# Routing product, row buffers, logits and FFN steps moved in a fused attention, FFN and expert kernel

## The chip, the cores and the metric

One core of a Trainium2 chip runs the kernel. The metric is the device time of one execution in microseconds (us), the median of several runs; a profiled execution of the same program gives the trace. Engines: PE (TensorE, matrix products), DVE (VectorE), ACT (ScalarE), POOL (GpSimd) and SP (SyncE, which only issues transfers).

## The reference

Three layers in a row, all in float32:

- Attention over `q`, `k`, `v` of shape 4 x 8 x 576 x 64: scores `q k^T / 8`; those under the row's maximum less `tau` are masked; softmax; times `v`. The result is laid out as 2304 tokens of 512 values.
- A dense FFN: `h = x @ w_in` (512 to 2048), `g = max(0.01 h, h)`, `x = g @ w_out`.
- A routed FFN: `logits = x @ w_gate + modality_bias[modality_id]` over 8 experts; each token goes to the expert with the largest logit, with that expert's softmax value as its gate: `out = gate * (relu(x @ w1[e]) @ w2[e])`, with 1024 hidden values.

## The kernel before, in words

The order of the instructions on each engine is written out by hand: every engine runs its own in program order and waits on semaphores where data comes from another engine. Products are made of a high and a low half of each float32 operand, so an operand is first copied (the high half, on ACT) and subtracted (the low half, on DVE or POOL).

**Attention** (`Attention`) goes over 16 pairs of heads in 9 steps each; a loop in `body` drives it. Products of probabilities and values (`pv`) come five steps late (`PVL`), and their evictions later still (`pv_out`: ACT in the following step, DVE in the one after), so there are some steps after the last score. Beside it `Units` runs the first part of the dense FFN for six blocks of 256 tokens, a few products per step (`start`, `mid`, `late`, `tail`), and `Moe1.convs` turns the dense weights into halves in small steps. What is left of the units at the end is run by `un.finish`, with one step of the weight conversion per round.

**The rest of the dense FFN** (`Tail`) is a list of items. An item is one slice of 128 hidden values: the first product `mm1` into `h`, the activation (`leaky`: ACT, DVE, ACT, DVE), and two items later (`LAG`) the second product `mm2` into `y`. First come blocks 6 to 8 with slices 0 to 5 (18 items), then all blocks with slices 6 to 15: blocks 0 to 7 in pairs, 512 columns wide (40 items), then block 8 alone (10 items). Then come two groups of 256 tokens of the most loaded experts (`turn` for tag `g`, 16 items), and after them the table-driven groups (`Groups`).

`pre` holds the steps to be done ahead of an item, by its place in the list: `fetch` asks SP for a block's rows of the attention result `xd` into the one buffer `un.xr`; `turn` transposes them on PE (`turned`, into PSUM tile `tp`) and makes the halves (`split_x`). `fetch_part` brings back the partial result of slices 0 to 5; for the last block that is done in `done1` itself, on SP, with the addition on DVE right behind.

**Routing** runs in the gaps. `extra` is a queue of generators; at each *place* (`advance`: between parts of `mm1`, after it, between parts of `mm2`, at the item's end; eight in a wide item, four in a narrow one) the first of them makes one step. `slowly(gen, k)` puts k places between two steps. When a block of `y` is done (`done1`), its logits and its routing are queued:

- blocks counted 1 to 6: `Route.logits`, 16 long vector operations with a running sum on DVE, one per place (`LD`);
- blocks 7 to 9: `Route.logits_mm`, eight transposes of `y` on PE into `ytp`, copies to `yT` (one on ACT, one on DVE; the tiles are `ct[2]` and `ct[0]`, of which `ct[0]` also serves the wide `leaky`), and 16 small product instructions into `lp`, with two places per step (`LG`);
- all: `Route.block`: the expert's one-hot row `hot` on DVE, then at the next place the product `rp` of `hot` with a triangle and with ones on PE (ranks and counts), then rank, gate and position `pi` on DVE, a store of `y` to `yd` on SP, and two scatters of token ids into `idt` from POOL, where the second waits for the first.

After block 9 `Route.table` makes the table of groups from the counts; its first group reads `idt` (`load_ids`), gathers rows of `yd` (`exg`) and is transposed on PE (`tp<-ident,exg`).

PSUM tag `u` has two buffers, which `tp`, `ytp`, `lp` and `rp` share in turn.

Of the kernel before, what the change touches and what calls it, by code (L numbers as in the profile page):

```python
# [31 lines left out]
GT = 256  # L32
# [423 lines left out]
class Route:  # L456
# [104 lines left out]
    def block(self, b, y, sb, ps, ps_tag):  # L561
# [23 lines left out]
        v.tensor_tensor(hot, per_e(self.w8), per_tile(fe), op=ALU.is_equal)  # L585
        yield
        rp = ps.tile([P, 512], F32, tag=ps_tag, name="rp")
# [14 lines left out]
        v.tensor_copy(pi, pf)  # L602
        nc.sync.dma_start(self.yd[b * GT:(b + 1) * GT, :].rearrange("(t p) c -> p t c", t=2), y)
        for t in range(2):
# [138 lines left out]
class Tail:  # L743
# [8 lines left out]
    def __init__(self, tc, ctx, mo, rt, un, w1, w2, out, wts):  # L752
# [8 lines left out]
        self.raw = itertools.cycle(self.raws).__next__  # L761
        self.xr1 = un.xr
        self.xh = itertools.cycle([un.xh, bp.tile([P, 4, GT], F32R, name="xh")]).__next__
# [31 lines left out]
    def fetch(self, b):  # L795
        self.mo.xload(b, self.xr1)

    def turn(self, key, rows, t, wide=False):
        if t == 0:
            self.xs = self.x5() if wide else (self.xh(), self.xl())  # L800
        elif t == (3 if wide else 1):
            self.x[key] = self.xs
        tp = self.pr.tile([P, 4, P], F32, tag="u", name="tp")
        turned(self.tc.nc, rows[:, t % 2], tp, self.rt.ident)
        for _ in split_x(self.tc.nc, tp, *self.xs, t):
            pass
# [12 lines left out]
    def done1(self, b, ys, part):  # L819
        nc = self.tc.nc  # L820
        yt = self.yt()
        for t in range(2):
            if part == 2:
                nc.vector.tensor_tensor(yt[:, t, 0:DM], ys[t], self.xgs[b % 2][:, t, 0:DM], op=ALU.add)
            elif part:
                nc.sync.dma_start(yt[:, t, 0:DM], self.mo.yp[2 * b + t])
                nc.vector.tensor_tensor(yt[:, t, 0:DM], ys[t], yt[:, t, 0:DM], op=ALU.add)
            elif t == 0:
                nc.vector.tensor_copy(yt[:, t, 0:DM], ys[t])
            else:  # L830
                nc.scalar.activation(yt[:, t, 0:DM], ys[t], AF.Copy)
        if self.blocks == 0:
            self.rt.load_wide(self.raws[2:])
        self.blocks += 1
        if self.blocks == 1:
            self.extra.append(iter([None] * 12))
        if self.blocks <= NB - 3:
            self.extra.append(slowly(self.rt.logits(yt, self.sb, f(self.cts[2])), LD[self.blocks - 1]))
        else:
            self.extra.append(slowly(self.rt.logits_mm(yt, self.yT, self.pr, "u"), LG))  # L840
        self.extra.append(slowly(self.rt.block(b, yt, self.sb, self.pr, "u"), RB[self.blocks - 1]))
        if self.blocks == NB - 3:
            self.extra.append(self.rt.early(self.sb1))
            self.extra.append(self.routed())
        elif self.blocks == NB:
            self.extra.append(self.rt.table(self.sb2()))
# [62 lines left out]
    def ahead(self, g, p):  # L909

        a = [(0, 0, lambda: self.load_ids(g)), (p - 7, 1, lambda: self.gather(g)),
             (p - 2, 3, lambda: self.turn(("g", g), self.xg[g], 0)), (p - 1, 3, lambda: self.turn(("g", g), self.xg[g], 1))]
        def load(q):
# [291 lines left out]

LG = 2

# [5 lines left out]
LAT = ["678", "457"]  # L1213
RB = [1] * 9
LD = [1]*8
FL = [0, 2, 3, 4]
# [146 lines left out]
def body(tc, qkt, vt, tau, win, wout, mid, wg, wgt, mb, w1, w2, out):  # L1363
    nc = tc.nc
    with ExitStack() as top, tc.manual_schedule():
# [12 lines left out]
        with ExitStack() as c1:  # L1378
# [12 lines left out]
            for w in steps:  # L1391
                if w == "conv":
                    pace += CV[n // 36]
                    while pace >= 1.0 and cv.n < 8 * NA:
                        next(cv)
                        pace -= 1.0
                elif n >= 36:
                    if w == "start" and n % 36 == LATE:
# [25 lines left out]
        ta.sb2 = lambda: groups().sb  # L1424
        bank[0] = itertools.cycle(ta.pys[2:4]).__next__
        un.finish(cv)
        items, pre = [], []
# [3 lines left out]
        for b in range(len(FB), NB):  # L1431
            p = len(items)
            pre += [(p - 5, 0, 0, lambda b=b: ta.fetch(b))] + [(p - 2 + t, 0, 0, lambda b=b, t=t: ta.turn(b, un.xr, t)) for t in range(2)]
            items += [item(b, fi, start=fi == 0, stop=fi == NA - 1, ys=ta.pys[0:2], done=(lambda ys, b=b: ta.done0(b, ys)))
                      for fi in range(NA)]
# [4 lines left out]
        for b in range(0, NB - 1, 2):  # L1440
            p = len(items)
            for k in range(2):
                pre += [(p - 4 + 2 * k, 0, 0, lambda b=b, k=k: ta.fetch(b + k)), (p + 5, 0, 0, lambda b=b, k=k: ta.fetch_part(b + k))]
                pre += [(p - 2 + k, 0, 0, lambda b=b, t=2 * k + t: ta.turn((b,), un.xr, t, True)) for t in range(2)]
            items += [dict(item(b, fi, start=fi == NA, stop=fi == NF - 1, nt=4, done=(lambda ys, b=b: both(b, ys))), x=(b,))
                      for fi in range(NA, NF)]
        items[(NB - len(FB)) * NA]["hook"] = lambda: bank.__setitem__(0, lambda: None)
        b, p = NB - 1, len(items)
        pre += [(p - 4, 0, 0, lambda: ta.fetch(b))] + [(p - 2 + t, 0, 0, lambda t=t: ta.turn((b,), un.xr, t)) for t in range(2)]
        items += [dict(item(b, fi, start=fi == NA, stop=fi == NF - 1, done=(lambda ys: ta.done1(b, ys, 1))), x=(b,)) for fi in range(NA, NF)]  # L1450
        p = len(items)
# [90 lines left out]
```

## Time and profile before

| | |
|---|---|
| median of 3 runs | 1055.83 us (1049.67 to 1056.2) |
| profiled execution | 1056.48 us, span of its instructions 1054.8 us |
| PE busy | 935.5 us, 89% of the span |
| DVE, ACT, POOL busy | 744.8, 587.7, 428.6 us |
| instructions | 20411 |
| HBM read, written | 118.88 MB, 19.79 MB |

A busy share is a mean over stages with different limits: attention ends near 400 us, the dense FFN near 765 us, and the groups fill the rest. The times in the rows below are from the span's start.

### The profile page before, as it was taken

What the parts mean: (1) busy time and instruction counts of PE and PEld (TensorE: products, weight loads), DVE (VectorE), ACT (ScalarE), POOL (GpSimd) and SP (SyncE); (2) the same over time, 40 slices, a digit from 0 to 9 for tenths busy, and PEclk for the clock granted to TensorE, in tenths of its full rate; (3) what the DMA queues carried; (4) which work ended last, traced back from release to release, by engine and by line L of the source; (5) the groups of instructions that cost most, each with busy time, mean ns of one, the idle gap of its engine ahead of it and who ended that gap; (6) DMA issues with size and microseconds to landing.
All of it is one profiled execution on the core that took longest, in us unless ns stands there. A gap on an engine that the chain in (4) does not pass through costs nothing. (4 is left out here: it accounts for less than half of the span.)

```text
span 1054.8 us, 20411 instructions
## 1 busy us (share of the span) xinstructions
PE 935.5 (89%) x7001; PEld 816.3 (77%) x7001; DVE 744.8 (71%) x1842; ACT 587.7 (56%) x1165; POOL 428.6 (41%) x514
## 2 busy tenths in 40 slices
PE   4666789999998997999998987989979999999984
PEld 3565678989897896888886875868868999998963
DVE  7898988989898873776368483684547666565574
ACT  6687888988887873654222212122335556564473
POOL 3899988898888861322000000010112211221121
PEclk9788899999999998999999998999989999999998
DMA  8999999999999884553032133042585988665572
GB/s 217 204 227 240 227 250 213 212 226 220 201 209 242 176 155 142 172 180 120 21 120 43 38 80 41 1 100 81 104 189 157 336 305 280 231 241 169 159 267 107
DMA packets 262874, 181.96 MB, mean 173 GB/s; under 512 B 186258, under 2 KB 223254, under 8 KB 262744
## 3 DMA queue, kind: packets, MB, share of 16 engines
q1 hardware_dynamic: 251696, 160.53, 62.8%
q0 software_dynamic: 4736, 12.92, 3.7%
q10 hardware_dynamic: 6312, 6.94, 2.1%
q8 instruction: 61, 1.00, 0.4%
q14 instruction: 69, 0.57, 0.2%
HBM read 118.88 MB, written 19.79 MB: 131 GB/s over the span
## 5 line engine op out<-in xcount | busy, mean ns | idle before, releaser
L196 POOL TENSOR_TENSOR p<-p,p 128x512 f16<-128x512 f32 x144 | 170.0, 1180 | 0.0
L150 PE MATMUL s<-khh,qs 128*128 128x288 f32 x320 | 105.6, 344 | 51.7 <-DVE p L175 28.5
L429 ACT ACTIVATE ct<-h 128x256 f32<-128x256 f32 (+1 forms) x104 | 48.3, 465 | 150.1 <-PE h L421 146.6
L453 PE MATMUL y<-w,g 128*128 128x512 f32 x480 | 130.3, 407 | 0.0
L158 DVE TENSOR_REDUCE s<-s 128x1 f32<-128x576 f32 x144 | 109.4, 759 | 26.2 <-PE s L223 23.3
L431 DVE SCALAR_TENSOR_TENSOR h<-h,ct 128x256 f32<-128x256 f32 (+1 forms) x104 | 55.3, 532 | 97.8 <-ACT ct L429 97.5
L453 PE MATMUL y<-w,w 128*128 128x512 f32 x480 | 124.3, 410 | 0.0
L175 DVE SCALAR_TENSOR_TENSOR p<-s,tb,e 128x576 f32<-128x576 f32 x144 | 117.3, 815 | 8.9 <-ACT e L167 4.4
L605 POOL DMA_INDIRECT idt<-ids,pi x18 | 17.8, 990 | 259.6 <-DVE pi L602 161.9
L421 PE MATMUL h<-w,w 128*128 128x512 f32 x480 | 120.4, 399 | 0.0
L150 PEld LDWEIGHTS s<-khh,qs 128*128 128x128 f32 x320 | 66.4, 208 | 61.2 <-DVE p L175 18.8
L222 PE MATMUL s<-vs,pt 128*128 128x128 bf16 (+1 forms) x680 | 109.2, 229 | 3.6 <-DMA pt<-p 3.5
L453 PEld LDWEIGHTS y<-w,w 128*128 128x128 f32 x480 | 93.6, 197 | 20.9
L167 ACT ACTIVATE e<-s,tb 128x576 f32<-128x576 f32 x144 | 107.1, 744 | 4.6 <-DVE tb L162 4.5
L421 PEld LDWEIGHTS h<-w,w 128*128 128x128 f32 x480 | 91.3, 191 | 21.6 <-DVE w L412 0.2
L223 PE MATMUL s<-vs,pt 128*128 128x64 bf16 (+1 forms) x680 | 104.1, 198 | 0.0
L194 ACT ACTIVATE p<-p 128x576 f16<-128x576 f32 x144 | 99.4, 690 | 4.9 <-DVE tb L162 4.1
L150 PE MATMUL s<-kll,qs 128*128 128x288 f32 x320 | 96.7, 316 | 0.0
L453 PEld LDWEIGHTS y<-w,g 128*128 128x128 f32 x480 | 85.6, 191 | 14.2
L225 PE MATMUL s<-vs,pt 128*128 128x128 bf16 (+1 forms) x544 | 90.1, 226 | 0.0
L421 PE MATMUL h<-uxh,w 128*128 128x256 f32 x448 | 88.6, 296 | 0.7 <-ACT uxh L410 0.7
L421 PE MATMUL h<-exh,w 128*128 128x256 f32 (+1 forms) x448 | 87.0, 290 | 0.7 <-ACT exh L410 0.7
(247 smaller groups left out, 2348.3 us busy)
## 6 DMA issues: line engine op xcount, KB each, us to landing
cr<-w SPq DMA_DIRECT2D x36, 512.0 KB
raw_qk<-qkt SPq DMA_DIRECT2D x30, 576.0 KB
raw<-w SPq DMA_DIRECT2D x24, 512.0 KB
ur<-xd SPq DMA_DIRECT2D x18, 512.0 KB
eraw<-w SPq DMA_DIRECT2D x18, 512.0 KB
cr<-w_in SPq DMA_DIRECT2D x16, 512.0 KB
cr<-w_out SPq DMA_DIRECT2D x16, 512.0 KB
ur<-w SPq DMA_DIRECT2D x12, 512.0 KB
```

Of the source, the lines that this page charges most:

```text
L150: nc.tensor.matmul(s[:, j, 0:288], qf[:, c0:c0 + P], x[:, j * 288:(j + 1) * 288], start=(k == 0), stop=(k == len(ops) - 1))
L158: v.tensor_reduce(self.mq[n], self.sq[n], axis=AX.XY, op=ALU.min)
L167: self.tc.nc.scalar.activation(e, self.sq[n], AF.Exp, bias=self.mq[n][:, 1:2], scale=-1.0)
L175: self.tc.nc.vector.scalar_tensor_tensor(p, self.sq.pop(n), self.mq.pop(n)[:, 0:1], self.eq.pop(n), op0=ALU.is_le, op1=ALU.mult, accum_out ...
L194: nc.scalar.activation(pp[:, 0:S], p, AF.Copy)
L196: nc.gpsimd.tensor_tensor(pp[:, S + D:], p[:, 0:4 * P], pp[:, 0:4 * P], op=ALU.subtract)
L222: nc.tensor.matmul(o[r0:r1, 0:2 * D], hi, v12, start=(c == 0), stop=False)
L223: nc.tensor.matmul(o[r0:r1, D:2 * D], hi, vs[:, h, c, 2], start=False, stop=(c == 4))
L225: nc.tensor.matmul(o[r0:r1, 0:2 * D], pt[:, 5 + c, r0:r1], v12, start=False, stop=False)
L421: nc.tensor.matmul(h, w[:, 0, a, s], b[:, c], start=(n == 0), stop=(n == 11))
L431: nc.vector.scalar_tensor_tensor(h, h, 0.01, a, op0=ALU.mult, op1=ALU.max)
L453: nc.tensor.matmul(y, a[:, s], w[:, 1, b], start=start and k == 0, stop=stop and k == 2)
```

## The change

- `Route.block`: three places instead of one between `hot` and the product `rp`; the store of `y` is issued by POOL instead of SP.
- Two buffers for the FFN's rows: `un.xr` and a weight tile, by the block's parity. Both fetches of a pair stand five items ahead (before: four and two). The fetch of block 6 is issued before `un.finish`.
- Blocks counted 2, 4 and 6 take their logits by `logits_mm` on PE, one place per step (`LG = 1`); blocks 7 to 9 do too, behind eight empty places each.
- No unit work in attention's last two steps (149 and 150); `un.finish` does it afterwards.
- `turn` is split into `turn`, `turn_g` and `turn_in`, and `RB` and `LD` become plain numbers of the same value.

```diff
@@ Route.block
         v.tensor_tensor(hot, per_e(self.w8), per_tile(fe), op=ALU.is_equal)
-        yield
+        for _ in range(3):
+            yield
         rp = ps.tile([P, 512], F32, tag=ps_tag, name="rp")
...
-        nc.sync.dma_start(self.yd[b * GT:(b + 1) * GT, :].rearrange("(t p) c -> p t c", t=2), y)
+        nc.gpsimd.dma_start(self.yd[b * GT:(b + 1) * GT, :].rearrange("(t p) c -> p t c", t=2), y)
@@ Tail.__init__
-        self.xr1 = un.xr
+        self.xrs = [un.xr, f(self.raws[1]).rearrange("p (t c) -> p t c", t=2)]
@@ Tail
     def fetch(self, b):
-        self.mo.xload(b, self.xr1)
-
-    def turn(self, key, rows, t, wide=False):
+        self.mo.xload(b, self.xrs[b % 2])
+
+    def turn(self, b, t, wide=False):
+        key, rows = ("x", b // 2) if wide else b, self.xrs[b % 2]
+        t += 2 * (b % 2) if wide else 0
         if t == 0:
             self.xs = self.x5() if wide else (self.xh(), self.xl())
         elif t == (3 if wide else 1):
             self.x[key] = self.xs
+        self.turn_in(rows[:, t % 2], t)
+
+    def turn_g(self, g, t):
+        if t == 0:
+            self.xs = self.xh(), self.xl()
+        else:
+            self.x["g", g] = self.xs
+        self.turn_in(self.xg[g][:, t], t)
+
+    def turn_in(self, row, t):
         tp = self.pr.tile([P, 4, P], F32, tag="u", name="tp")
-        turned(self.tc.nc, rows[:, t % 2], tp, self.rt.ident)
+        turned(self.tc.nc, row, tp, self.rt.ident)
         for _ in split_x(self.tc.nc, tp, *self.xs, t):
             pass
@@ Tail.done1
-        if self.blocks <= NB - 3:
-            self.extra.append(slowly(self.rt.logits(yt, self.sb, f(self.cts[2])), LD[self.blocks - 1]))
+        if self.blocks <= NB - 3 and self.blocks % 2:
+            self.extra.append(slowly(self.rt.logits(yt, self.sb, f(self.cts[2])), LD))
         else:
+            if self.blocks > NB - 3:
+                self.extra.append(iter([None] * 8))
             self.extra.append(slowly(self.rt.logits_mm(yt, self.yT, self.pr, "u"), LG))
-        self.extra.append(slowly(self.rt.block(b, yt, self.sb, self.pr, "u"), RB[self.blocks - 1]))
+        self.extra.append(slowly(self.rt.block(b, yt, self.sb, self.pr, "u"), RB))
@@ module
-LG = 2
+LG = 1
-RB = [1] * 9
-LD = [1]*8
+RB = 1
+LD = 1
@@ body
-                elif n >= 36:
+                elif 36 <= n < 9 * B * HP + PVL:
                     if w == "start" and n % 36 == LATE:
                         un.add(2 * (n // 36 - 1))
                     getattr(un, w)(n % 9)
...
         bank[0] = itertools.cycle(ta.pys[2:4]).__next__
+        ta.fetch(len(FB))
         un.finish(cv)
...
-            pre += [(p - 5, 0, 0, lambda b=b: ta.fetch(b))] + [(p - 2 + t, 0, 0, lambda b=b, t=t: ta.turn(b, un.xr, t)) for t in range(2)]
+            pre += [(p - 5, 0, 0, lambda b=b: ta.fetch(b))] if p else []
+            pre += [(p - 2 + t, 0, 0, lambda b=b, t=t: ta.turn(b, t)) for t in range(2)]
...
-                pre += [(p - 4 + 2 * k, 0, 0, lambda b=b, k=k: ta.fetch(b + k)), (p + 5, 0, 0, lambda b=b, k=k: ta.fetch_part(b + k))]
-                pre += [(p - 2 + k, 0, 0, lambda b=b, t=2 * k + t: ta.turn((b,), un.xr, t, True)) for t in range(2)]
+                pre += [(p - 5, 0, 0, lambda b=b, k=k: ta.fetch(b + k)), (p + 5, 0, 0, lambda b=b, k=k: ta.fetch_part(b + k))]
+                pre += [(p - 2 + k, 0, 0, lambda b=b, k=k, t=t: ta.turn(b + k, t, True)) for t in range(2)]
```

## Rows read from the trace of the kernel before

**Rows 1.** The page, part 1: busy us (share of the span) xinstructions.

```profile
PE 935.5 (89%) x7001; PEld 816.3 (77%) x7001; DVE 744.8 (71%) x1842; ACT 587.7 (56%) x1165; POOL 428.6 (41%) x514
```

**Rows 2.** Waits of PE from 390 us on: us in total, times, longest.

```profile
PE rp L590 <- DVE hot L585: 15.6, 7, 2.7
PE tp L405 <- DMA ur<-xd: 11.0, 3, 5.0
PE ytp L548 <- DVE yt L827: 6.8, 1, 6.8
```

**Rows 3.** Timeline of PE, 550 to 566 us: start, us, what, [idle before <-releaser].

```profile
551.18 2.96 PE L421 MATMUL h<-w,w 128*128 128x512 f32 x12
...
559.37 0.21 PE L590 MATMUL rp<-hot,tri 128*128 128x8 bf16 x2 [2.43 <-DVE hot L585]
...
559.51 4.59 PE L421 MATMUL h<-w,w 128*128 128x512 f32 x12
```

**Rows 4.** Windows: stretch, us, busy PE, PEld, DVE, ACT, POOL, clock, DMA share, GB/s.

```profile
555.00:645.00 90.00, 80.53 (x345) 64.08 (x344) 63.61 (x198) 17.33 (x33) 7.69 (x8) 0.92 0.24 53
685.00:765.00 80.00, 73.85 (x420) 62.99 (x419) 51.43 (x175) 21.99 (x49) 8.69 (x9) 0.98 0.42 95
466.60:473.80 7.20, 7.14 (x36) 5.96 (x37) 4.74 (x9) 4.31 (x9) 2.59 (x2) 1.00 0.43 146
409.00:416.20 7.20, 6.46 (x29) 5.87 (x30) 3.10 (x6) 3.05 (x6) 1.28 (x1) 0.53 0.42 151
656.80:664.00 7.20, 7.20 (x25) 6.07 (x26) 1.98 (x3) 1.68 (x3) 0.00 (x0) 0.64 0.00 0
779.50:786.70 7.20, 7.20 (x31) 6.34 (x32) 3.46 (x7) 2.71 (x7) 0.00 (x0) 0.63 0.62 156
```

**Rows 5.** Timeline of SP and PE around two fetches of rows.

```profile
462.50 0.37 SPq L399 DMA_DIRECT2D ur<-xd  x1
...
466.66 1.07 PE L405 MATMUL tp<-ident,ur 128*128 128x128 f32 x8 [1.34 <-DMA ur<-xd]
...
646.23 0.36 SPq L399 DMA_DIRECT2D ur<-xd  x1
...
656.80 1.94 PE L405 MATMUL tp<-ident,ur 128*128 128x128 f32 x8 [5.04 <-DMA ur<-xd]
```

**Rows 6.** Timeline of PE, block 7's logits product.

```profile
739.31 1.85 PE L558 MATMUL lp<-wg,ct 128*128 128x8 f32 x16
```

**Rows 7.** Timeline of SP, DVE and PE, the last block, 762 to 830 us.

```profile
767.20 0.89 SPq L826 DMA_DIRECT2D yt<-yp  x2
...
778.74 1.41 DVE L827 TENSOR_TENSOR yt<-y,yt 128x512 f32<-128x512 f32 x2 [6.49 <-DMA yt<-yp]
...
779.48 1.11 PE L548 MATMUL ytp<-ident,yt 128*128 128x128 f32 x4 [6.82 <-DVE yt L827]
...
784.05 0.69 DVE L552 COPY ct<-ytp 128x512 f32<-128x512 f32 x1 [0.70 <-PE ytp L548]
```

**Rows 8.** Timeline of PE, ACT and SP, end of attention, 390 to 412 us.

```profile
399.28 5.12 PE L453 MATMUL y<-w,g 128*128 128x512 f32 x21
...
401.25 0.31 ACT L251 ACTIVATE xs<-s,rs 128x64 f32<-128x64 f32 x1 [0.40 <-ACT ct L1288]
...
404.40 0.36 SPq L399 DMA_DIRECT2D ur<-xd  x1
...
409.05 1.67 PE L405 MATMUL tp<-ident,ur 128*128 128x128 f32 x8 [4.65 <-DMA ur<-xd]
```

**Rows 9.** Tile `idt`: duration ns min/median/max, first and last start.

```profile
L605 POOL DMA_INDIRECT idt<-ids,pi x18: 954/958/1202, 560.9 to 800.9; - x18
```

**Rows 10.** Timeline of POOL and PE, from the last scatter to the first table group.

```profile
800.87 0.98 POOL L605 DMA_INDIRECT idt<-ids,pi  x1 [5.92 <-DMA idt<-ids,pi]
...
811.55 1.03 POOL L1050 DMA_INDIRECT exg<-yd,eid  x1 [0.30 <-issue]
...
820.57 0.60 PE L405 MATMUL tp<-ident,exg 128*128 128x128 f32 x4
```

More of the change, by code (lines that the diff above doesn't have):

```diff
@@ L911, in ahead @@
         a = [(0, 0, lambda: self.load_ids(g)), (p - 7, 1, lambda: self.gather(g)),
-             (p - 2, 3, lambda: self.turn(("g", g), self.xg[g], 0)), (p - 1, 3, lambda: self.turn(("g", g), self.xg[g], 1))]
+             (p - 2, 3, lambda: self.turn_g(g, 0)), (p - 1, 3, lambda: self.turn_g(g, 1))]
         def load(q):
@@ L1442, in body @@
             for k in range(2):
-                pre += [(p - 4 + 2 * k, 0, 0, lambda b=b, k=k: ta.fetch(b + k)), (p + 5, 0, 0, lambda b=b, k=k: ta.fetch_part(b + k))]
-                pre += [(p - 2 + k, 0, 0, lambda b=b, t=2 * k + t: ta.turn((b,), un.xr, t, True)) for t in range(2)]
-            items += [dict(item(b, fi, start=fi == NA, stop=fi == NF - 1, nt=4, done=(lambda ys, b=b: both(b, ys))), x=(b,))
+                pre += [(p - 5, 0, 0, lambda b=b, k=k: ta.fetch(b + k)), (p + 5, 0, 0, lambda b=b, k=k: ta.fetch_part(b + k))]
+                pre += [(p - 2 + k, 0, 0, lambda b=b, k=k, t=t: ta.turn(b + k, t, True)) for t in range(2)]
+            items += [dict(item(b, fi, start=fi == NA, stop=fi == NF - 1, nt=4, done=(lambda ys, b=b: both(b, ys))), x=("x", b // 2))
                       for fi in range(NA, NF)]
@@ L1448, in body @@
         b, p = NB - 1, len(items)
-        pre += [(p - 4, 0, 0, lambda: ta.fetch(b))] + [(p - 2 + t, 0, 0, lambda t=t: ta.turn((b,), un.xr, t)) for t in range(2)]
-        items += [dict(item(b, fi, start=fi == NA, stop=fi == NF - 1, done=(lambda ys: ta.done1(b, ys, 1))), x=(b,)) for fi in range(NA, NF)]
+        pre += [(p - 4, 0, 0, lambda: ta.fetch(b))] + [(p - 2 + t, 0, 0, lambda t=t: ta.turn(b, t)) for t in range(2)]
+        items += [item(b, fi, start=fi == NA, stop=fi == NF - 1, done=(lambda ys: ta.done1(b, ys, 1))) for fi in range(NA, NF)]
         p = len(items)
```

## The prediction

> **What bounds the kernel now.** I read the page first: TensorE (PE) is busy for 89% of the span, more than any other engine [rows 1]. From attention's end on it runs one FFN product behind another, so what counts there is where PE stands still. So the second view is PE's list of waits from 390 us to the end. Three entries hold 33.4 us: the routing product `rp` waits for `hot` on DVE (15.6 us in seven stops), the transposes `tp` of the FFN's rows wait for the transfer of those rows (11.0 us in three), and the last block's transposes `ytp` wait for an addition on DVE (6.8 us, one stop) [rows 2]. The third view is PE's timeline around such a stop: 12 products take 2.96 us ahead of one and 4.59 us behind it [rows 3]. That is the clock: the windows behind the stops show a granted share under 1.00 [rows 4], that is, part of them at 1.2 instead of 2.4 GHz. A stop is paid for twice, then.
>
> Nearly every edit aims at one of these three entries. I cost the parts in us of the profiled execution (1056.5, 0.7 over the median), a gain positive. A "place" is a point where one step of background work is put between products; in the wide stage three 128x512 products lie between two places. One product is 2.96/12 = 0.247, so a place is 0.74 [rows 3].
>
> **Routing product two places further on** (the third after `hot`, it was the first): 2 x 0.74 = 1.48 of products now run ahead of it. Blocks 1, 3 and 5 keep their logits on DVE, so `hot` comes no earlier: a stop of 2.43 becomes 0.95 [rows 3], and two stops of at most 2.7 become 1.2 each [rows 2]. At the other blocks nothing is left: the even ones reach `hot` sooner (below), and for block 8 I count its stop as gone. Left: 0.95 + 1.2 + 1.2 = 3.4; gain 15.6 - 3.4 = **12.2**. The vector work behind `rp` (rank, count, position) moves back by the same two places; nobody but the scatter of the ids waits for it.
>
> **The clock behind these stops.** 90 us at 0.92 and 80 us at 0.98 [rows 4] make 7.2 + 1.6 us lost; with the rounding of two digits I take **8.5**. Stops near 1 us remain. The nearest row is the one of 1.34 us at 466.66 [rows 5], and the window behind it shows 1.00 [rows 4], so I count no fall there. If each of the three remaining ones costs a fall, about 1.6 each (4.59 - 2.96) [rows 3], 4.9 of it is lost again.
>
> **Logits of blocks 2, 4 and 6 on PE.** Each adds eight transposes and the products `lp`. Eight transposes of the same form take 1.07 [rows 5], `lp` of block 7 takes 1.85 [rows 6]: 3 x 2.9 = 8.8, somewhat less since ends overlap; I take **-8** (-7 to -8.8). This is on the path, since PE is the bound. What it buys is that DVE has no 16 long products ahead of `hot`; the transposes' copies, one on ACT and one on DVE, lie in engines with room. The new wait is that of `lp` for DVE's copy: it is issued two places (1.48) after the transposes, the copy takes 0.69 [rows 7], and DVE has no logits then, so I count no stop; at the other end, 1 us a block. ACT's next write of the shared `ct` tile waits for `lp`; its consumer on PE is two items later, so nobody is late. Taken alone this part costs about what it brings.
>
> **End of attention.** The eviction of an FFN block stands ahead of the last attention tile's on ACT: that one starts at 401.25 behind it, while PE goes on to the FFN at 399.28, done with attention [rows 8]. Without FFN work in the two last steps it can start about 1.7 earlier. The stores and the fetch of the next rows (issued at 404.40) follow from it, so the fetch goes out near 402.7. It is also ahead of a weight load in SP's queue now. Before, it took 4.65 from issue to its transposes; the fetch at 462.50 took 4.16 [rows 5, 8]. Rows at 402.7 + 4.2 = 406.9; PE runs dry at 409.05 - 4.65 = 404.4 as before, because its products keep their order. Idle 2.5 instead of 4.65: 2.1. The window behind shows 0.53 of 7.2 us, a loss of 3.4 [rows 4]; one fall of 1.6 stays: 1.8. Together **3.9** (1.7 if only the start moves, 8 if the stop goes). The FFN steps left out run later with a step of the weight conversion beside each; those fill engines that wait for the fetch anyway. On SP the weight loads now stand behind the fetch's wait for the stores, which ends about when the first of them went before.
>
> **Two buffers for the rows.** The second fetch of a pair no longer waits until the first block's transposes have freed the only buffer. At 646.23 it went out just then and PE stood 5.04 [rows 5]; with both issued five items ahead that is hidden under some 30 us of products. With the clock behind it (0.36 x 7.2 = 2.6 [rows 4]): **7.6**. The stop at 466.66 gives **1.3** [rows 5]. The second buffer is a weight tile that this stage doesn't use otherwise.
>
> **The last block.** Its partial rows are asked for at 767.20 and DVE adds at 778.74; PE stands 6.8 [rows 2, 7]. Eight empty places, less one for the halved spacing, put seven places ahead of `ytp`. They hold two second products, a first one and half of the next, equal to 21 products of 512 columns: 5.2. The stop falls to 1.6. But DVE is held in order by that addition and then owes two items' work before the copy that `lp` needs; even before, with one item, the copy ended at 784.7, and PE would be there at 779.5 + 1.1 + 0.7 + 1.5 = 782.8 [rows 3, 5, 7]. So 1.9 comes back: gain 6.8 - 3.5 = 3.3, and the clock's 2.7 (0.37 x 7.2 [rows 4]) shrinks to 1.6: **4.4** (1 to 8).
>
> **The late route.** The last `rp` is six places later in PE's order (eight empty and two for `rp`, less four by the halved spacing), so 4.4 us less product work lies between it and the first table group; and the `y` store now stands on POOL ahead of the scatters, where issuing one takes 0.95 to 1.2 [rows 9]. The second scatter waits 5.92 for the first; the gathers start at 811.55 and PE uses the first at 820.57 without waiting [rows 10]. Nine us minus a transfer of 4.2 to 4.65 [rows 5, 8] leaves under 5 of slack, and 5.5 is eaten. I take **-2** (0 to -9, all of those nine). Taking the store off SP frees the weight loads queued behind it there; no wait of PE hung on these, so nothing is counted.
>
> **Sum.** 12.2 + 8.5 - 8 + 3.9 + 7.6 + 1.3 + 4.4 - 2 = 27.9. From the median, 1055.8 - 27.9 = 1027.9: **1028**. All bounds at their best give 1017, all at their worst (clock 3.6, logits -8.8, end of attention 1.7, last block 1, late route -9) 1046.
>
> **Rivals.** *The stops move on.* DVE's backlog stays in blocks 1, 3, 5, and PE meets it at the next low half that DVE owes: half of the 12.2 and 4.9 of the clock are lost, 1028 + 11 = 1039. For it speaks that these logits issue one long product per place, as long as the place; against it, that PE needs a low half only two items later. *The fetches were not held by the buffer*, but by slow transfers: then the 3.9 and 7.6 don't come, 1039.5; the one at 646.23 took 10 us to arrive. Against it, five items ahead covers even that. In this form the change would not do what it says. *Slower.* The `y` store on the software queue lands at the scatter's pace. A scatter of 128 rows took 0.98 + 5.92 = 6.9 [rows 10]; 256 rows at that pace are 13.8, and the stores of blocks 7, 8 and 9 stand ahead of six scatters in series, on which the ids of the first table group wait: 3 x 13.8 less about 4 of slack is 37, and two clock losses of 2.7 make 1028 + 43 = 1071. It decides from about 10 us a store. Against it: the gathers from 811.55 on carry such long rows, and the first is used 9 us later without a wait [rows 10].
>
> The Trainium skill has a rule that speaks against that store: "SBUF — State Buffer", section "SBUF: two separate sides", says that a DMA issued from GpSimd gets its descriptors from GpSimd's cores, which are shut out while DVE runs certain copies, and advises the other queues. The trace shows no sign of it: 18 scatters were issued in 954 to 1202 ns between busy DVE work [rows 9]. By the rule each of three stores would wait for a copy of 0.69 [rows 7], giving 1030.
>
> **Chances.** Forecast (1018 to 1038) 0.70; stops moving on, 0.13; fetches not recovered, 0.07; slower 0.04; the rest, losses adding up near no gain, 0.06. About 1% is what a measurement of this kernel can tell from no change (before: 1049.7 to 1056.2). Faster by over 1% takes in the first three nearly whole: 0.87; within 1%: 0.09; slower: 0.04. The range runs from 1018 to 1045 and leaves out about 0.15.
>
> **What would show it.** In the new profile: `rp` waiting for `hot` 3 to 4 us in all; no wait of `tp` for rows at the pair starts, and one of 2 to 3 us after attention; `ytp` waiting for the addition 1 to 2 us and `lp` for a copy near 2; `lp` in six blocks instead of three; few windows under 1.00 between 400 and 790 us; a first transposition of the table group with up to 3 us of idle. Wrong it would be if stops of 2 us remain at `rp`, if half clock follows stops of 1 us, or if PE waits at the first table group for 10 us.

## The result and the profile after

The changed kernel took 1042.07 us (median of 8 runs, 1036.29 to 1045.03), the kernel before 1055.53 beside it (8 runs). The ratio is 0.9885, 95% interval [0.9845, 0.9925]: 13.5 us gained between the medians, where 27.9 were forecast. The execution profiled after took 1042.11, its span is 1040.3.

The page of the kernel after, part 1 (answers [rows 1]), and its list of waits of PE from 390 us on (answers [rows 2]):

```profile
PE 934.5 (90%) x7073; PEld 818.0 (79%) x7073; DVE 716.6 (69%) x1749; ACT 590.6 (57%) x1168; POOL 433.6 (42%) x523
```

```profile
PE tp L405 <- issue: 7.1, 3, 4.5
PE tp L405 <- DMA exg<-yd,eid: 4.9, 1, 4.9
PE rp L591 <- DVE hot L585: 3.6, 3, 1.3
PE h L421 <- DVE g L440: 2.5, 1, 2.5
PE tp L405 <- DMA ur<-xd: 2.1, 1, 2.1
```

The three entries that held 33.4 us [rows 2] hold 8.2 now: `rp` 3.6, the rows' fetch 2.1, and in place of `ytp` a product `h` that waits 2.5 for `g`. On top stand two stops that were not there: 4.5 us in the first entry (the other two of its three are old ones of 1.1 and 1.5 us near 955 and 993 us) and 4.9 at the table group. The clock is the second thing to read. The stretch from the first FFN products to the last block, in the kernel before and in the kernel after:

```profile
417.00:757.00 340.00, 316.77 (x1562) 262.27 (x1560) 215.77 (x557) 103.87 (x209) 40.72 (x35) 0.97 0.32 86
```

```profile
417.00:757.00 340.00, 333.62 (x1751) 279.22 (x1749) 194.80 (x486) 113.82 (x230) 46.11 (x43) 1.00 0.32 93
```

Up to 757 us the change did what it should: the clock share went from 0.97 to 1.00, and PE is busy for 333.6 of 340 us instead of 316.8. So most of what is missing lies behind that. These are starts of PE instructions in the two timelines, less the start of the first transposes after attention (409.05 before, 408.31 after), since that one lies some 5 us apart from one execution to the next (405.8 to 411.1 in those of the kernels with the change):

```
PE comes to                          before   after    gained
first group's transposes  (tp<-xg)    350.6   328.3     22.3
second group's transposes (tp<-xg)    387.1   366.2     20.9
table group's transposes  (tp<-exg)   411.5   396.3     15.2
```

With 0.7 us more at the attention's fetch this is a gain of 23 us at the first group. At the table group it is 16, and half clock behind that stop takes 2 more (the next transposes of this group stand 5.4 us behind the first, 3.3 before). Not all of the 23 is saved: the second of the last three blocks (counted 8) has its logits and routing product ahead of the first group's transposes before (its `rp` at 757.10) and behind them after (its `lp` at 741.87). A kernel below that puts them ahead again comes to that mark 2.8 us later. What happens in between is read from POOL. First the kernel before, POOL and PE:

```profile
744.74 0.99 POOL L605 DMA_INDIRECT idt<-ids,pi  x1 [3.14 <-DVE pi L602]
...
776.32 0.98 POOL L868 DMA_INDIRECT xg<-yd,ids  x1 [0.30 <-issue]
...
796.16 0.60 PE L405 MATMUL tp<-ident,xg 128*128 128x128 f32 x4
```

Then POOL in the kernel after, from block 7's store to the table group's gather:

```profile
731.24 0.76 POOL L604 DMA_DIRECT2D yd<-yt  x1 [7.75 <-DVE pf L601]
732.31 1.01 POOL L606 DMA_INDIRECT idt<-ids,pi  x1 [0.30 <-DVE h L431]
741.38 0.97 POOL L606 DMA_INDIRECT idt<-ids,pi  x1 [8.06 <-DMA idt<-ids,pi]
749.02 0.76 POOL L604 DMA_DIRECT2D yd<-yt  x1 [6.66 <-DVE pf L601]
753.83 0.98 POOL L606 DMA_INDIRECT idt<-ids,pi  x1 [4.05 <-DMA idt<-ids,pi]
764.80 0.96 POOL L606 DMA_INDIRECT idt<-ids,pi  x1 [9.99 <-DMA idt<-ids,pi]
766.07 0.99 POOL L883 DMA_INDIRECT xg<-yd,ids  x1 [0.30 <-DVE oh L577]
...
775.04 1.02 POOL L606 DMA_INDIRECT idt<-ids,pi  x1 [4.14 <-DMA idt<-ids,pi]
786.89 0.97 POOL L606 DMA_INDIRECT idt<-ids,pi  x1 [10.82 <-DMA idt<-ids,pi]
...
797.78 0.99 POOL L1065 DMA_INDIRECT exg<-yd,eid  x1 [7.13 <-DMA eid<-idt]
```

And PE, DVE and SP beside it, in the kernel after:

```profile
744.48 0.85 SPq L839 DMA_DIRECT2D yt<-yp  x2
...
756.76 0.69 DVE L840 TENSOR_TENSOR yt<-y,yt 128x512 f32<-128x512 f32 x1 [5.38 <-DMA yt<-yp]
...
758.46 0.80 PE L421 MATMUL h<-uxh,w 128*128 128x256 f32 x2 [2.46 <-DVE g L440]
...
774.51 0.63 PE L405 MATMUL tp<-ident,xg 128*128 128x128 f32 x4 [4.50 <-issue]
...
804.61 1.08 PE L405 MATMUL tp<-ident,exg 128*128 128x128 f32 x4 [4.90 <-DMA exg<-yd,eid]
```

The second group's gather of `xg` stands in POOL's order behind the four scatters of blocks 7 and 8, as it did before, and a scatter waits for the landing of the one before it. Before, that gather went out at 776.32 and PE used its rows at 796.16, 20 us later and without waiting. After, it goes out at 766.07, 10.3 us earlier; PE is there at 770.01, 26.2 us earlier than before, and stands 4.5 us (the list writes "issue", since it has no event of the landing; the tile says what it reads). The rows are used 8.4 us after the issue. If they took that long before, too, 11.4 of the 20 us were slack, while PE gained 15.9 on the gather; the difference is the stop of 4.5. Two more chains end late beside it: the last block's partial rows, asked for at 744.48 behind weight loads and added at 756.76, and the last block's own scatters, with the table's gather at 797.78 behind them.

### The profile page after: what moved, and what is told of

The parts are those of the page before. It is cut to its first block, busy times and chain, and to the rows that moved or that the text cites. A ratio compares the mean times of both kernels' runs of the same rounds, so it can differ in the third digit from the quotient of the medians.

```text
span 1040.3 us, 20475 instructions
## 1 busy us (share of the span) xinstructions
PE 934.5 (90%) x7073; PEld 818.0 (79%) x7073; DVE 716.6 (69%) x1749; ACT 590.6 (57%) x1168; POOL 433.6 (42%) x523
## 5 line engine op out<-in xcount | busy, mean ns | idle before, releaser
L150 PE MATMUL s<-khh,qs 128*128 128x288 f32 x320 | 104.9, 342 | 49.8 <-DVE p L175 27.9
L453 PE MATMUL y<-w,w 128*128 128x512 f32 x480 | 119.2, 395 | 0.0
L421 PEld LDWEIGHTS h<-w,w 128*128 128x128 f32 x480 | 89.2, 188 | 22.9 <-ACT w L410 1.3
L453 PEld LDWEIGHTS y<-w,w 128*128 128x128 f32 x480 | 88.9, 188 | 19.1
L222 PEld LDWEIGHTS <-pt 128*128 128x128 f16 (+1 forms) x680 | 68.9, 104 | 18.2 <-DMA pt<-p 7.3
```

The lines of the kernel that those rows point to most:

```text
L150: nc.tensor.matmul(s[:, j, 0:288], qf[:, c0:c0 + P], x[:, j * 288:(j + 1) * 288], start=(k == 0), stop=(k == len(ops) - 1))
L222: nc.tensor.matmul(o[r0:r1, 0:2 * D], hi, v12, start=(c == 0), stop=False)
L421: nc.tensor.matmul(h, w[:, 0, a, s], b[:, c], start=(n == 0), stop=(n == 11))
L453: nc.tensor.matmul(y, a[:, s], w[:, 1, b], start=start and k == 0, stop=stop and k == 2)
```

## The experiments

All numbers are medians with the ratio to the kernel before that ran on the same chip and its 95% interval. The experiments ran on several chips, on which the kernel before had medians from 1050.4 to 1055.5, so the ratios compare better than the medians. Where the intervals of two experiments overlap, the times don't tell the two apart, so I also give the stretch **A**: from PE's first transposes after attention to the table group's first ones. It is 411.5 before and 396.3 after. It comes from one execution of each kernel.

**First: the store's queue and the empty places.** Four kernels, for two theories: S, that the store of `y` holds the scatters behind it on POOL's queue; P, that the eight empty places ahead of the logits of blocks 7 and 8, too, push the scatters back. The edits, in this order (`e3_store_idle` has the first two together):

```diff
-        nc.gpsimd.dma_start(self.yd[b * GT:(b + 1) * GT, :]...
+        nc.sync.dma_start(self.yd[b * GT:(b + 1) * GT, :]...
...
-            if self.blocks > NB - 3:
+            if self.blocks == NB:
                 self.extra.append(iter([None] * 8))
...
-             (p - 7, 1, lambda: self.gather(g)),
+             (p - (10 if g else 7), 1, lambda: self.gather(g)),
```

Expected of the store on SP's queue: 

> The changed kernel with the store of y back on SP. In the changed kernel PE stands 4.5 us at the second group's transposes (tp<-ident,xg) and 4.9 us at the table group's (tp<-ident,exg), with half clock behind both. Theory S (the store on POOL's queue holds the scatters behind it): both waits go, some 9 us and 4 us of clock, so about 1030 us. Theory P (the empty places move the scatters of blocks 7 and 8 so late that the gather behind them in POOL's order and the last block's scatters are late): both waits stay within 1 us, time 1042 plus or minus 3.

Of empty places ahead of block 9 alone: 

> The changed kernel with the eight empty places ahead of the last block's logits alone, not of blocks 7 and 8. Theory P: the scatters of block 8 come eight to sixteen places (6 to 12 us) earlier, the gather behind them too, so the wait of 4.5 us goes; the last block's first scatter no longer waits 4.1 us for block 8's, so of 4.9 us less than 1 is left: about 1032 us. Theory S: the waits stay, 1042 plus or minus 3.

Of both: 

> Both edits at once: store of y on SP, empty places ahead of the last block alone. Either theory: no wait over 1 us at either group, about 1030 us. If one of the edits alone gives the same, that one was the cause; if each gives half, both were.

Of the second group's gather three items earlier: 

> The changed kernel with the second group's gather three items earlier in the list, which puts it ahead of block 8's store and scatters in POOL's order. Both theories: the 4.5 us at the second group go, since the rows it reads are long stored; if they stay, the gather was held by the transfers themselves. The table group's wait of 4.9 us stays or grows, since PE comes there earlier: 1036 to 1042 us.

Measured: 1040.57 (0.9872 [0.9827, 0.9917], A 393.3), 1041.75 (0.9878 [0.9835, 0.9921], A 393.2), 1037.1 (0.9824 [0.9778, 0.9871], A 395.5) and 1045.54 (0.9915 [0.9885, 0.9945], A 398.4). Neither theory's 1030 came. Waits of PE from 417 to 811 us, the store on SP's queue:

```profile
PE tp L405 <- issue: 5.7, 1, 5.7
PE rp L591 <- DVE hot L585: 3.6, 3, 1.3
PE h L421 <- DVE g L440: 3.5, 1, 3.5
```

The same, with places ahead of block 9 alone:

```profile
PE h L421 <- DVE g L440: 4.9, 1, 4.9
PE tp L405 <- DMA exg<-yd,eid: 4.1, 1, 4.1
PE rp L591 <- DVE hot L585: 3.6, 3, 1.3
```

The same, with the gather early:

```profile
PE h L421 <- DVE g L440: 9.8, 1, 9.8
PE tp L405 <- DMA exg<-yd,eid: 5.8, 1, 5.8
```

Each edit by itself removes one of the three stops, and what PE wins there it loses at another: without the places the second group's stop is gone and the one for the last rows has doubled. An early gather carries the rows in time; it is issued at 743.46, just as the last block's rows are asked for (744.36), and PE then waits 9.8 us for the work behind these. The first two edits together don't remove two stops: the execution of `e3_store_idle` in the trace has 5.6 us at the second group, 5.3 at the table group and 1.5 for `g`. It was the longest of four (1034.97 to 1044.56), so what the two do together stays open. Theory P is borne out at the second group; for theory S only the table group's stop speaks, and the time doesn't. There are three late arrivals one behind the other.

**Second: the last block's rows, the places, the scatters.** `e5_early_y` asks for the last block's partial rows seven items after that block's start, `e6_early_y_no_places` also drops the empty places, `e13_no_places` drops only these:

```diff
+    def fetch_last(self, b):
+        self.last = self.yt()
+        for t in range(2):
+            self.tc.nc.sync.dma_start(self.last[:, t, 0:DM], self.mo.yp[2 * b + t])
...
-        yt = self.yt()
+        yt = self.last if part == 1 else self.yt()
...
-                nc.sync.dma_start(yt[:, t, 0:DM], self.mo.yp[2 * b + t])
...
+        pre += [(p + 7, 0, 0, lambda: ta.fetch_last(b))]
...
-            if self.blocks > NB - 3:
-                self.extra.append(iter([None] * 8))
```

`e7_one_scatter` leaves out one of the scatters (`for t in range(1 if b == NB - 2 else 2)`).

Expected, early rows: 

> Changed kernel, except that the last block's partial rows are asked for seven items after that block's start, ahead of weight loads of the first group, instead of after its last product (744.48 us, addition held until 756.76). Two theories of where the gain is given back between 745 and 825 us. Theory L (late rows): the addition that waits for these rows holds the DVE and starts the last block's routing 10 us late. By it the stop of 2.46 us at 758 goes, the last block's scatters come 5 to 8 us earlier and the stop of 4.87 us at the table group goes with the half clock behind it (3.4 us): 1042 - 2.5 - 4.9 - 3.4 = 1031 us; the stop of 4.5 us at the second group stays. Theory C (chain of scatters): six scatters one behind the other, each waiting 8 to 12 us for the landing of the one before, set both stops. By it TensorE only comes to the second group's transposes earlier and waits there: 1042 us, that stop 7 us instead of 4.5.

Early rows and no places: 

> Changed kernel with the early request for the last block's rows and without the eight empty places ahead of the last three blocks' logits. Theory L: no stop over 2 us is left between 745 and 800 us and the table group's goes: 1042 - 2.5 - 4.5 - 4.9 and about 5 us of half clock = 1026 us. Theory C: the places only moved the first scatter of each block; the scatters are as far apart as before, so the second group's gather comes about 5 us earlier (as in the kernel with places ahead of the last block alone, where it was issued at 760.5 instead of 766.1) and the table group's stop stays at 4 to 5 us: 1036 us.

No places: 

> Changed kernel without the eight empty places ahead of the last three blocks' logits, the last block's rows asked for as late as in it. Theory L (the addition that waits for these rows sets the last block's scatters): the second group's stop goes (4.5 and 1.7 of half clock) but the stop ahead of it stays or grows to 5 and the table group's stays: 1040 us, as with places ahead of the last block alone (1041.75). If the places did the harm by themselves: 1036 us, as with the early request.

One scatter less: 

> Changed kernel that leaves out the second of the two scatters of the block before the last (128 token numbers less in the lists). Theory C: the second group's gather leaves GpSimd some 10 us earlier (about 755 instead of 766), its stop of 4.47 us and the half clock behind it (1.7) go, the last block's first scatter no longer waits for a landing (4.1), so the table group's stop falls by 4 us less the 6 us by which TensorE comes earlier: about 1036 us, with a table stop of 5 to 7 us. Theory L: the second group's gather isn't what binds; the stop at 758 us, for the last block's rows, grows instead or the table group's stop takes all that is won: 1041 us.

Measured: early rows 1041.19 (0.9885 [0.9829, 0.9941], A 395.5), no places 1037.56 (0.9878 [0.9811, 0.9945], A 393.9), both 1036.05 (0.9839 [0.9786, 0.9892], A 386.8), one scatter less 1037.05 (0.9831 [0.9774, 0.9888], A 391.0). Waits of PE with the early rows alone, 400 to 811 us:

```profile
PE tp L405 <- issue: 12.3, 1, 12.3
```

With no places alone:

```profile
PE ytp L548 <- DVE yt L840: 10.7, 1, 10.7
```

With both:

```profile
PE tp L405 <- DMA exg<-yd,eid: 3.9, 1, 3.9
PE rp L591 <- DVE hot L585: 3.6, 3, 1.3
```

Either edit alone leaves one stop of 11 to 12 us in place of three; both leave 3.9, and A falls by 9.5. The times are less clear: the intervals of all four overlap with that of the changed kernel. Theory C had the second group right. The table group's stop went with the early rows alone, as theory L said, but mostly because PE was held longer at the second group: counted from the first transposes, the table's gather leaves at 388.1, only 1.4 us earlier than in the changed kernel (389.5). With the places gone the late rows do show: it leaves at 384.9 without early rows and at 380.1 with them. So the two causes hide each other: the scatters of blocks 7 and 8 set the second group, and where these are out of the way, the late rows set the last block's scatters and the table group. The kernel with one scatter less supports the first half, its second group doesn't stand (its list from 400 us on has 5.3 at the table group and 2.8 for `g`), as theory C said and theory L didn't.

**Third: the parts of the change by themselves.** `e8_logits_dve` puts the even blocks' logits back on DVE, `e9_before_rp` is the kernel before with the routing product's two places alone, `e10_one_buffer` the changed kernel with one row buffer, `e11_ffn_last_steps` with FFN work in attention's last steps:

```diff
-        if self.blocks <= NB - 3 and self.blocks % 2:
+        if self.blocks <= NB - 3:
...
(in the kernel before)
-        yield
+        for _ in range(3):
+            yield
         rp = ps.tile([P, 512], F32, tag=ps_tag, name="rp")
...
-        self.xrs = [un.xr, f(self.raws[1])...]
+        self.xrs = [un.xr, un.xr]
-                pre += [(p - 5, 0, 0, lambda b=b, k=k: ta.fetch(b + k)), ...
+                pre += [(p - 4 + 2 * k, 0, 0, lambda b=b, k=k: ta.fetch(b + k)), ...
...
-                elif 36 <= n < 9 * B * HP + PVL:
+                elif n >= 36:
```

Expected, logits on DVE: 

> Changed kernel with the logits of the 2nd, 4th and 6th block back on VectorE. Undoes one part. The prediction put that part at 8 us of TensorE time for three blocks (16 products of 0.12 us and two sets of transposes each). If TensorE is what binds there, these 8 us come off at 700 us; if VectorE then holds the routing product (stops of 1.0 to 1.3 us at 557, 610 and 672 us become 3 to 5 us, as before the change for the first of them), the two cancel. By theory C, whatever is won by 700 us is given back at the second group: 1040 to 1043 us. By the prediction's sum: 1034 us.

The routing product alone: 

> Kernel before with one part of the change alone: the routing product three places later instead of one. The prediction's terms for it: stops of 15.6 us fall to 3.4 (12.2 gained) and the half clock behind them goes (8.5): 1055 - 20.7 = 1034 us if nothing is given back later. The rival that the stops move on (VectorE still holds the product, or the next wait) gives 1045 us. If the end of the routing chain binds (theory C: six scatters of 8 to 12 us each), some 8 to 10 us are given back at the second group and the table group: 1043 us.

One buffer: 

> Changed kernel with one row buffer instead of two, and the fetches of the pairs at their old places. The prediction's term for the two buffers: 7.6 us at the pairs' fetches (the stop of 5.04 and its half clock) and 1.3 at the first ones. If TensorE arrives that much later at the second group, less is given back there: by theory C 1042 + 9 - 6 = 1045 us; by the prediction's sum 1051 us.

FFN work in the last steps: 

> Changed kernel with FFN work again in attention's last two steps. The prediction's term: 3.9 us (2.1 of the stop at the fetch, 1.8 of half clock). In the profile after, attention itself ended 1.8 us later and the stop was 2.07 instead of 4.65, a net of 0.7 by 408 us. By the term: 1046 us if what is won there lasts to the end. By the profile's ledger, and with what is given back at the second group: within 1 us of the changed kernel.

Measured: 1035.68 (0.9824 [0.9761, 0.9887], A 388.5), 1046.02 (0.9896 [0.9803, 0.9989], A 398.6), 1048.5 (0.9959 [0.9926, 0.9992], A 402.3) and 1042.85 (0.9884 [0.9813, 0.9954], A 395.7). With the logits on DVE, waits of PE from 400 us on:

```profile
PE rp L591 <- DVE hot L585: 5.6, 6, 1.3
PE tp L405 <- issue: 5.3, 1, 5.3
PE tp L405 <- DMA exg<-yd,eid: 2.8, 1, 2.8
PE h L421 <- DVE g L440: 2.4, 1, 2.4
```

The part that moved the logits buys 2.0 us of stops at `rp` (3.6 instead of 5.6) and costs PE about 7.5: four transposes twice and `lp` in three blocks. With DVE doing them PE comes from its first transposes to those of the last block (counted 9) in 290.1 us instead of 295.6: 5.5 less. That is what the time shows, too: 6.4 us by the medians, though the two intervals overlap. Theory C expected this to be given back at the second group, 1040 to 1043; it wasn't, since the gather there comes 5.5 us earlier as well (352.3 behind the first transposes instead of 357.8).

The two places alone bring `rp` to 5.7 us from 15.6, and A falls by 12.9 of the 20.7 us that the prediction's two terms for them add up to; stops of 2.2 and 1.5 us stand at the second and the table group. The time, with its wide interval, is nearer to theory C's 1043 than to 1034. With one buffer the time lies between the two expectations; three stops for rows are back, and one of 1.0 us in the first products:

```profile
PE tp L405 <- DMA ur<-xd: 6.4, 3, 3.9
PE rp L591 <- DVE hot L585: 3.6, 3, 1.3
...
PE h L421 <- issue: 1.0, 1, 1.0
```

The FFN work in attention's last steps makes the fetch's stop 4.2 instead of 2.1; the time doesn't tell the two apart.

**Fourth: traffic, and whether the losses add.** `e14_half_weights` leaves out 6 of the first two groups' 16 weight loads, `e16_no_weights` all 16 (the `dma_start` lines of `load_w`; the groups multiply by what the buffers hold). `e12_early_no_places_dve` joins early rows, no places and logits on DVE, `e15_best_store_sp` adds the store on SP's queue.

Expected, some weights left out: 

> Changed kernel that leaves out three of four loads of the second weight matrix of the first two groups (6 of 16 loads of 512 KB between 720 and 790 us). Theory T (traffic): the scatters of the last three blocks stand 10 to 12 us apart because weights are on the DMA engines, and 7 to 8 us apart without (at 560 to 700 us of the changed kernel); with fewer weights the spacing falls to 8, the last block's rows land in under 9 us instead of 12, and the stops of 2.46, 4.47 and 4.87 us go or fall to half: 1033 us. Theory F (fixed): the spacing is that of a scatter and its wait alone and stays at 10 to 11: 1041 us.

All left out: 

> Changed kernel that leaves out all 16 weight loads of the first two groups (512 KB each; the groups multiply by what the buffers hold). With 6 of 16 left out the DMA share of 740 to 770 us was 0.67 instead of 1.00 and four distances between scatters had a mean of 10.0 us instead of 11.4; between 560 and 700 us, at shares of 0.13 to 0.26, a pair stands 7 us apart. Theory T (traffic): with no weights the pairs stand 7 us apart here too, the second group's gather leaves GpSimd at about 756 instead of 766, its stop and the table group's go: 1042 - 2.5 - 4.5 - 4.9 and 2 to 3 of half clock = 1028 us. Theory F (fixed by the stage, as by the 516 KB store of each block ahead of them): 10 us apart, 1039 us as with 6 left out.

The three edits: 

> Changed kernel with three edits: the last block's partial rows asked for early, no empty places ahead of the last three blocks' logits, and the 2nd, 4th and 6th block's logits back on VectorE. If the routing chain's end and TensorE's work for those logits are two separate losses, they add: 1036 (the first two edits alone) less 6 (the third alone) = 1030 us. If what the third edit wins before 700 us is given back at the table group, whose stop of 3.8 us then grows to 9: 1036 us.

The three and the store: 

> The kernel with all three edits and the store of the finished rows back on SP's queue. If the store of 516 KB on the same queue as the scatters holds them: the spacing in the last two blocks falls by 2 to 4 us and the table group's stop with it: 1026 us. If it doesn't (one look at the store alone moved less than the intervals tell): 1030 us, no change against the three edits.

Measured: 1039.01 (0.9877 [0.9809, 0.9946], A 394.5), 1034.79 (0.9791 [0.9721, 0.9861], A 387.8), 1028.56 (0.9795 [0.9726, 0.9864], A 385.1), 1026.18 (0.9759 [0.9692, 0.9826], A 385.4). With some weights left out theory T's 1033 didn't come: the second scatters of blocks 7 to 9 wait 9.4, 8.7 and 6.4 us, the table group's stop is gone, and the second group's has grown to 9.8. Without weights, POOL's second scatters of blocks 7, 8 and 9:

```profile
742.80 0.97 POOL L606 DMA_INDIRECT idt<-ids,pi  x1 [8.65 <-DMA idt<-ids,pi]
...
760.16 0.96 POOL L606 DMA_INDIRECT idt<-ids,pi  x1 [7.14 <-DMA idt<-ids,pi]
...
777.92 0.97 POOL L606 DMA_INDIRECT idt<-ids,pi  x1 [7.34 <-DMA idt<-ids,pi]
```

The waits are 8.7, 7.1 and 7.3 instead of 8.1, 10.0 and 10.8 in the kernel after. So weights on the DMA engines cost some 3 us in each of two pairs, in these two executions; the last pair waits only 6.3 in the kernel with early rows, too, which loads all weights, but there it falls in a stretch with a DMA share of 0.02. The second group still stands 5.4 us without any weight. Theory T is right on the direction, and its 1028 is 7 us short. The experiment changes one thing more: without weight loads ahead of it on SP the request for the last block's rows goes out at 735.48 instead of 744.48, so it can't price the traffic alone. Nothing speaks for the store of 516 KB ahead of the scatters as the rest: on SP's queue the waits didn't fall (with three edits and the store there, they are 12.1 and 12.0 for blocks 7 and 8, 6.2 for block 9), between 560 and 700 us of the kernel after pairs right behind such a store stand only 6.8 to 7.1 us apart, and the 2.4 us between the last two kernels lie within their intervals. What sets the waits of 7 us stays open.

By the times the losses add, within the intervals: 1036.05 less 6 was expected, 1028.56 came. The traces don't show it so: what the logits' edit wins ahead of the first group it gives back at the second one, as its rival said of the table group. From the first transposes PE comes to

```
                              first group   second group   table group
the changed kernel                  328.3          366.2         396.3
logits on DVE                       322.8          360.1         388.5
early rows and no places            331.1          358.6         386.8
the three edits                     325.7          359.2         385.1
```

The rest of the difference between the last two lies ahead of the first transposes and behind the table group, in one execution each, and is not explained here. With the store on SP's queue the kernel is faster than the kernel before and than the changed one, its interval lies under the latter's. Waits of PE, 417 to 811 us, of that last one:

```profile
PE tp L405 <- issue: 6.5, 1, 6.5
PE rp L591 <- DVE hot L585: 5.6, 6, 1.3
```

Beside the `rp` stops one is left, at the second group, behind the scatters of blocks 7 and 8, though the empty places are gone. (The kernel without the store's edit has 5.9 there.)

## Why the prediction fell short, point by point

**Routing product: right.** 3.4 us were to be left, 3.6 are, in the three odd blocks. **The clock: right.** No fall behind the stops of 1.0 to 1.3 us, and the share over 340 us is 1.00. **Two buffers: right.** 8.9 forecast with the clock; with one buffer the time is 6.4 us longer, and the two intervals just miss each other.

**Logits on PE: size right, worth wrong.** 8 were put on PE's path and some 7.5 are there. But "taken alone this part costs about what it brings" fails: it brings 2.0, because two more places ahead of `rp` had already covered the DVE's logits. I costed the two edits one after the other and gave the stops that remain in even blocks (2.0 together) to this one at their old size.

**End of attention: half.** Idle 2.5 forecast, 2.1 found; in every kernel with this part the stop is 2.0 to 2.5, in the two without it that ran as experiments 4.2 and 5.0. But only 0.7 of the 3.9 shows at the transposes. Attention itself ended 1.8 us later in this execution (PE goes on to the FFN at 401.09 instead of 399.28; it is 399.08 in `e1_store_sp` with this part and 400.58 in `e11_ffn_last_steps` without it), and most of the clock's 1.8 didn't come: the window behind the stop, in the kernel after, still shows 0.61 of 7.2 us.

```profile
408.30:415.50 7.20, 6.41 (x31) 5.89 (x32) 3.48 (x7) 2.93 (x6) 1.28 (x1) 0.61 0.78 283
```

**Last block: the right cause at another instruction.** I had 1.6 us at `ytp` and 1.9 at `lp`. The stop is 2.46 at a product `h`, because DVE, held in order by the addition, owed it `g`.

**The late route: the step that failed.** Up to the first group's transposes 25.5 us were forecast (all terms but the last two) and 23 came, 2.8 of which is work moved behind them. Behind them +2.4 was forecast and about -9 came, or -6 without the moved work. The two stops at the groups are 4.5 and 4.9 us, and the 7.2 us behind them (from 774.5 and from 804.6) show clock shares of 0.76 and 0.68. So of the 14 us that are missing this step holds 8 to 9; the terms ahead of it hold the rest, 3.2 of it at attention's end. The term "-2 (0 to -9)" looked at the last block and the table group alone: I counted the eight places in front of block 9 and never asked what the same places in front of blocks 7 and 8 delay. Their scatters stand ahead of the second group's gather in POOL's order, and that gather isn't in the prediction at all. It also took the slack at the table group as it stood in the trace of before, with PE 20 us later, and it took too much: it put the way of the gathered rows at 4.2 to 4.65, as for other rows, and they took 6.8 (from 797.78 to 804.61), which leaves some 2 of the 9 us and not under 5. The trace of `e6_early_y_no_places` shows what the step cost: from the first group's transposes to the table group's PE takes 60.9 us before, 68.0 in the kernel after and 55.7 with places and late rows gone (A less the time to the first group). That is 12.3 us back, at the price of 2.8 ahead of the first group, where block 8's logits and routing product stand again: 9.5 in all. In the time it is 6.0 by the medians, and the intervals overlap.

**The rivals.** The stops at `rp` didn't move on, the fetches were held by the buffer. The slower one, a store at the scatter's pace, isn't there: the store on either queue gives the same time within the intervals. Nor did the rule of the Trainium skill show ("SBUF — State Buffer", section "SBUF: two separate sides"): the three stores of blocks 7 to 9 were issued in 0.76 to 0.79 us. That is no test of it, though: the Trainium skill speaks there of copies from SBUF to SBUF, and the copy of 0.69 us that the prediction priced reads `ytp` in PSUM.

## What to carry to other kernels

When an edit brings the bounding engine forward by 20 us, list every arrival that it meets further on, with its slack in the old trace, and subtract. Slack is the time from issue to use less what the transfer takes: of 20 us at the second group only 11 were slack. Ask of an empty place put ahead of one step who else stands behind that step in every in-order queue. Where several late arrivals follow each other, removing one can show nothing in the total: remove them together, and read a stretch of the trace beside it.

## What the runs showed of the hardware

A scatter of 128 numbers that waits for the one before it stands 6.5 to 7.9 us behind it in the six pairs between 560 and 700 us of the kernel after, at DMA shares of 0.00 to 0.23, and 9.1 to 11.9 in the three pairs behind 730 us, at shares of 0.40 to 0.87 (732.31 to 741.38, 753.83 to 764.80, 775.04 to 786.89), although it moves half a KB. The share isn't all of it: with places ahead of block 9 alone the first of these three pairs stands 8.9 us apart at a share of 0.23.

The clock doesn't follow the length of a stop alone. Between 417 and 757 us stops of 1.0 to 1.3 us are followed by full clock. In the table groups a stop of 1.1 us and one of 0.7 soon after it stand in two kernels at the same place in the program. In the kernel with early rows (951.89) half clock follows, the second of these windows:

```profile
950.80:954.60 3.80, 1.91 (x10) 1.39 (x11) 0.69 (x1) 1.75 (x3) 0.05 (x1) 1.00 0.94 302
954.60:958.00 3.40, 3.40 (x12) 3.40 (x11) 0.44 (x1) 0.96 (x3) 1.98 (x2) 0.50 0.97 355
```

In the kernel after (956.20) it stays full, with PE as busy ahead of it:

```profile
955.10:958.90 3.80, 1.90 (x10) 1.38 (x11) 0.69 (x1) 1.76 (x3) 0.03 (x1) 1.00 0.96 271
958.90:962.30 3.40, 3.40 (x21) 3.40 (x20) 1.43 (x3) 1.53 (x3) 2.00 (x2) 1.00 0.98 357
```

So what a single stop of this kind costs in clock can't be read off its length.
